# Block-sparse attention folded into a split-precision MoE feed-forward: attention in whole units of eight heads, placed by a plan in quarters of a step

## The chip, the cores and the metric

One NeuronCore of a Trainium2 chip runs the whole kernel. The metric is the device time in microseconds of one execution; the runs before the change have a median of 816.5 us (814.67, 816.5 and 819.2). The profiled execution took 815.99 us, and its trace spans 814.3 us; the 1.69 us between the two lie outside the trace. TensorE's granted clock averaged 0.986 of its full speed in it.

## The reference, cut to what matters

```python
batch, n_heads, seq, head_dim = (4, 8, 768, 64)      # 24 blocks of 32 positions
scores = scale * np.matmul(q, k.transpose(0, 1, 3, 2))
mask = np.abs(blk_i - blk_j) <= 1                    # neighbours
mask = mask | (blk_i == 0) | (blk_j == 0) | (blk_i == n_blocks - 1) | (blk_j == n_blocks - 1)
for qb in range(n_blocks):                           # and three sampled blocks
    for kb in sampled_blocks[qb]:
        mask[qb * block:(qb + 1) * block, kb * block:(kb + 1) * block] = True
scores = np.where(mask, scores, -1000000000.0)
scores = scores - np.max(scores, axis=-1, keepdims=True)
attn = np.exp(scores)
attn = attn / (np.sum(attn, axis=-1, keepdims=True) + 1e-09)
attn_out = np.matmul(attn, v)
x = attn_out.transpose(0, 2, 1, 3).reshape(B * S, H * D)      # 3072 x 512
h = x @ w_in                                         # 512 -> 2048
g = h * (1.0 / (1.0 + np.exp(-1.702 * h)))
return g @ w_out                                     # 2048 -> 512
```

Rows of blocks 1 to 22 see at most eight blocks of keys (first, last, three neighbours, three sampled). Rows of blocks 0 and 23 see all 768 keys.

## The kernel before, in words

**Units and chunks.** A unit is 64 positions of one batch element with all eight heads, held as four pairs of heads. A sparse unit is two neighbouring blocks out of 1 to 22; there are 44. A dense unit is blocks 23 and 0 of one batch element; there are four, and in the order of the 48 units they are numbers 22, 23, 46 and 47. Eight units make a chunk of 512 tokens, the width of one matmul of the MoE, and there are six chunks.

**The MoE step.** For each chunk there are 16 steps, 96 in all. A step does 12 matmuls up (L471 to L473: x and the 128 columns of w_in are each split in a rounded high part and a remainder, and three products of the parts are kept), then ScalarE's tanh (`g`, L479) and VectorE's product (L480), then 12 matmuls down for the step before (L508, L509 and L514), which accumulate over the 16 steps in four PSUM banks. In the first 16 steps `conv`, a generator, also turns the raw weights into such parts on ScalarE and VectorE, seven pieces to a step; afterwards w_out is loaded again in each step (`wst`) and split (L459, L460).

**Attention beside it.** A list of attention steps is worked off. A sparse step is half a unit (four heads): `scores` is 8 matmuls (L260) into banks 0 and 1, then one reduction by VectorE for each bank, which also scales, adds the mask and finds the extreme of each row (L279), and one exponential by ScalarE for each bank, which also sums (L292). A dense step is one head of each of two pairs: four matmuls of 384 keys (L271), reductions, a joint extreme `nmd`, exponentials. `transposes` turns the weights by TensorE (L307, L315) into the same two banks, and ScalarE copies them out as `pt` (L320). `values` multiplies by v into bank 2 (L338, L345). At a unit's end `normalise` scales on VectorE (`x`, L358), and `turn` transposes x (L368) and writes it as `xhi` and `xlo` (L373, L374) into the next chunk's input.

**Order.** The program is written by hand and each engine runs its instructions in that order; nothing reorders them. `tick` writes one MoE step together with the attention steps that are due: scores of step t, values of step t-2, then the 12 matmuls up, then the transposes of step t-1, then the matmuls down. `run` first writes all 16 attention steps of chunk 0, and two more, without MoE steps around them (the prelude, to about 77 us); then, by `goal`, it spreads the steps of chunk c+1 evenly over the 16 MoE steps of chunk c. Where a chunk has more than 16 attention steps (20, in the chunks with dense units) four MoE steps get two attention steps each, both ahead of the matmuls up. In the prelude the banks are others (`early`: scores in 0, 1 or 4, 5, transposes in 3 or 7, or 1 or 5 for a dense one, values in 2 or 6). Keys and values are prefetched in rings of two buffers by SyncE's and GpSimd's queues (`loads`); a buffer is loaded anew once the last step that reads it is written.

## Time and profile before

| what | value |
|---|---|
| median of three runs | 816.5 us |
| profiled execution, its span | 815.99 us, 814.3 us |
| TensorE (PE) busy | 768.3 us, 94% |
| VectorE (DVE), ScalarE (ACT) busy | 50%, 47% |
| DMA | 128.22 MB, 157 GB/s on average |

The page lists busy time by engine, slices of the span, DMA queues, the chain of work that ended last and the costliest groups. A matmul row's duration is longer than its share of the engine, since successive matmuls overlap: what one costs is read from the start of one row to the start of the next. A fp32 matmul of the attention is two instructions in the trace, so that eight score matmuls stand there as x16.

### The profile page before, as it was taken

How to read it: one execution, taken by the hardware profiler on the slowest of the kernel's cores; microseconds unless marked ns; L12 is line 12 of the kernel's file. 1: busy time of each engine (PE TensorE's matmuls, PEld its weight loads, DVE VectorE, ACT ScalarE, POOL GpSimd, SP SyncE). 2: the span in 40 equal slices, each digit the busy share in tenths (PEclk: the TensorE clock that was granted, in tenths of full speed). 3: DMA queues.
4: the chain of work that ended last, by engine and by line, in shares of the span. 5: the costliest groups of instructions: out<-in, count | busy, mean ns of one | idle time of the engine just before them, and what ended most of it. 6: DMA issues, size and time to landing. Idle time of an engine off the chain costs nothing.

```text
span 814.3 us, 19274 instructions
## 1 busy us (share of the span) xinstructions
PE 768.3 (94%) x7584; PEld 567.7 (70%) x7584; DVE 410.7 (50%) x1080; ACT 381.5 (47%) x933; POOL 55.8 (7%) x85
## 2 busy tenths in 40 slices
PE   3677999999999999999999999999999999999996
PEld 1344777777676767777777777777767667788885
DVE  3476788886444444454443544444544444343332
ACT  2476566665444444454444444444544444342332
POOL 5122101000000000000000000000000000000000
PEclk9699999999999999999999999999999999999999
DMA  8999777875734253774453463543654332031112
GB/s 265 313 303 323 216 255 236 258 249 164 210 124 150 66 194 119 202 212 118 118 157 116 134 204 104 154 132 117 167 158 151 115 88 90 27 91 53 49 42 53
DMA packets 61117, 128.22 MB, mean 157 GB/s; under 512 B 7569, under 2 KB 26514, under 8 KB 60514
## 3 DMA queue, kind: packets, MB, share of 16 engines
q1 hardware_dynamic: 46882, 80.50, 33.2%
q0 software_dynamic: 7232, 25.51, 9.7%
q10 hardware_dynamic: 6912, 20.97, 7.9%
q8 instruction: 60, 0.98, 0.5%
q14 instruction: 31, 0.25, 0.1%
HBM read 116.47 MB, written 10.49 MB: 156 GB/s over the span
## 4 chain that ended last, share of the span: by engine, by line
PE 84%; DVE 4%; ACT 4%; DMA 3%; issue 2%; SPq 1%; ACTq 0%; DVEq 0%
PE bank L471 12%; PE bank L508 10%; PE bank L509 10%; PE bank L473 10%; PE bank L472 10%; PE bank L514 10%; PE bank L260 5%; PE bank L338 5%; PE bank L307 4%; PE bank L271 3%; ACT ex L292 2%; DMA raw<-in_moe_w_in_dram 2%; PE bank L345 1%; PE bank L315 1%; PE bank L368 1%
## 5 line engine op out<-in xcount | busy, mean ns | idle before, releaser
L480 DVE SCALAR_TENSOR_TENSOR g<-g,bank 128x512 f32<-128x512 f32 x96 | 66.0, 687 | 233.2 <-ACT g L479 233.2
L471 PE MATMUL bank<-xhi,win 128*128 128x512 f32 x384 | 159.3, 415 | 0.0
L508 PE MATMUL bank<-wout,ghi 128*128 128x512 f32 x384 | 158.4, 412 | 0.0
L509 PE MATMUL bank<-wout,ghi 128*128 128x512 f32 x384 | 151.2, 394 | 0.0
L473 PE MATMUL bank<-xhi,win 128*128 128x512 f32 x384 | 150.3, 391 | 0.0
L292 ACT ACTIVATE ex<-bank,nm 128x256 f32<-128x256 f32 x176 | 81.9, 471 | 145.8 <-DVE nm L279 145.5
L472 PE MATMUL bank<-xlo,win 128*128 128x512 f32 x384 | 149.9, 390 | 0.0
L479 ACT ACTIVATE g<-bank 128x512 f32<-128x512 f32 x96 | 57.3, 597 | 163.3 <-PE bank L473 159.5
L514 PE MATMUL bank<-wout,glo 128*128 128x512 f32 x360 | 98.2, 394 | 0.0
L460 DVE TENSOR_TENSOR wout<-wst,wout 128x512 fp32r<-128x512 f32 x80 | 55.4, 692 | 76.5 <-ACT wout L459 76.5
L471 PEld LDWEIGHTS bank<-xhi,win 128*128 128x128 f32 x384 | 72.0, 187 | 19.7
L260 PE MATMUL bank<-kg,qt 64*32 64x256 f32 x1408 | 64.2, 412 | 20.8 <-DMA vmid<-in_v_dram 10.8
L473 PEld LDWEIGHTS bank<-xhi,win 128*128 128x128 f32 x384 | 72.1, 188 | 16.5
L279 DVE CUSTOM_DVE_ANT_1 bank<-bank,bias 128x256 f32<-128x256 f32 x176 | 71.5, 448 | 22.0 <-PE bank L260 9.6
L508 PEld LDWEIGHTS bank<-wout,ghi 128*128 128x128 f32 x384 | 72.4, 189 | 13.6
L509 PEld LDWEIGHTS bank<-wout,ghi 128*128 128x128 f32 x384 | 72.5, 189 | 13.3
L338 PEld LDWEIGHTS bank<-vown,pt 128*32 128x32 f32 x1408 | 45.7, 113 | 51.0 <-issue 18.4
L472 PEld LDWEIGHTS bank<-xlo,win 128*128 128x128 f32 x384 | 72.3, 188 | 12.6
L514 PEld LDWEIGHTS bank<-wout,glo 128*128 128x128 f32 x360 | 67.6, 188 | 16.0
L217 POOL DMA_INDIRECT vown<-in_v_dram,vidx x44 | 42.5, 965 | 521.1 <-PE bank L338 405.5
L338 PE MATMUL bank<-vown,pt 128*32 128x64 f32 x1408 | 61.1, 228 | 10.8 <-ACT pt L320 10.3
L485 ACT CAST ghi<-g 128x512 fp32r<-128x512 f32 x96 | 59.7, 621 | 20.3 <-DVE g L480 20.1
(71 smaller groups left out, 876.7 us busy)
## 6 DMA issues: line engine op xcount, KB each, us to landing
wst<-ws SPq DMA_DIRECT2D x80, 256.0 KB
kg<-in_kb_dram SPq DMA_DIRECT2D x136, 128.0 KB
kg<-in_kb_dram SPq DMA_DIRECT2D x22, 384.0 KB
raw<-in_moe_w_in_dram ACTq DMA_DIRECT2D x16, 512.0 KB
raw<-in_moe_w_out_dram ACTq DMA_DIRECT2D x16, 512.0 KB
kg<-in_kT_dram SPq DMA_DIRECT2D x4, 1536.0 KB
vown<-in_vd_dram SPq DMA_DIRECT2D x8, 768.0 KB
qt<-in_q_dram SPq DMA_DIRECT2D x22, 256.0 KB
```

What stands on the lines that cost most here:

```text
L260: nc.tensor.matmul(sps[h][BLK * c:BLK * (c + 1), 0:n].rearrange("p (n s) -> p n s", s=BLK), self.qt[r][rows, bi, UT * pair + BLK * j:UT * ...
L279: nc.vector.tensor_tensor_reduce(out=at, in0=at, in1=bias, scale=-SCALE, scalar=3.0e38, op0=ALU.add, op1=ALU.min, accum_out=nm[:, c:c + 1])
L292: nc.scalar.activation(out=ex, in_=sms[c], func=AF.Exp, bias=least[c], scale=-1.0, accum_out=sums[c])
L338: nc.tensor.matmul(av[BLK * c:BLK * (c + 1), 2 * i + h], pt[:, 2 * h + k, BLK * c:BLK * (c + 1)], src[:, at:at + D], start=(k == 0), stop= ...
L471: nc.tensor.matmul(h, wih[:, k], hi[:, k], start=(k == 0), stop=False)
L472: nc.tensor.matmul(h, wih[:, k], lo[:, k], start=False, stop=False)
L473: nc.tensor.matmul(h, wil[:, k], hi[:, k], start=False, stop=(k == NCT - 1))
L480: nc.vector.scalar_tensor_tensor(out=g, in0=g, scalar=1.0, in1=self.h, op0=ALU.add, op1=ALU.mult)
L485: self.nc.scalar.copy(out=ghi, in_=self.g[m][0])
L508: nc.tensor.matmul(o[n], ghi[:, tk[n]], woh, start=(f == 0), stop=False)
L509: nc.tensor.matmul(o[n], ghi[:, tk[n]], wol, start=False, stop=False)
L514: nc.tensor.matmul(o[n], glo[:, tk[n]], woh, start=False, stop=False)
```

## The change: what it does

1. An attention item is now a whole sparse unit (all eight heads) or, of a dense unit, two pairs of heads with one half of the keys (384). There are 44 sparse items and 16 dense ones. A sparse item's 16 score matmuls are written together, its 32 value matmuls together, its 8 transposes together. Of its two banks, one holds the first heads of the pairs and the other the second, both full (512 columns).
2. The four score matmuls of a dense item go to both halves of the array's rows: its h runs over both heads of a pair, where a step before had one. Each half of the keys is exponentiated with its own extreme; `factors` then brings the two halves of a row to a common extreme (five small VectorE operations and one small exponential), and `normalise` scales both halves of the values and adds them (three operations of 128x256 for a dense unit, where there was one).
3. `plan` gives each item a start in quarters of an MoE step: quarter 0 ahead of the matmuls up, 1 in their middle, 2 behind them, 3 inside the matmuls down. At its start an item's scores are written, and behind them the values of the item before; its transposes follow four quarters later (two for a dense item), with the `turn` of the unit before. Sparse items start every 8 quarters (two steps) in most chunks, every 6 or 8 in the first 14 steps, every 5 or 6 beside dense units; dense items every 4.
4. The prelude (`first`) holds chunk 0's eight items and no part of the ninth; for item n it writes the values of n-2, the scores of n, the turn of n-2 and the transposes of n-1. In it scores alternate between banks 0, 1 and 4, 5, and transposes use 3 and 7 always.
5. `up` and `down` can be written in two parts; `down` keeps the order of its matmuls. Loads are asked for after each quarter.

PE at a dense item, before (here h = 0 of two pairs; bank 0 is the first half of the keys and bank 1 the second, and x2 are the two pairs):

```order
L514 MATMUL bank6_91<-wout1_118,glo_4318 128x512
L271 MATMUL bank0_85<-kg0_93,qt0_95 64x384 x2
L271 MATMUL bank1_86<-kg0_93,qt0_95 64x384 x2
L345 MATMUL bank2_87<-vown1_98,pt_4365 64x64 x6
L345 MATMUL bank2_87<-vown1_98,pt_4366 64x64 x6
```

The same place now (bank 0 is the first head of each pair, bank 1 the second, all of one half of the keys):

```order
L528 MATMUL bank6_91<-wout0_117,glo_3978 128x512
L272 MATMUL bank0_85<-kg0_93,qt0_95 64x384
L272 MATMUL bank1_86<-kg0_93,qt0_95 64x384
...
L336 MATMUL bank2_87<-vown0_97,pt_4081 64x64 x6
L336 MATMUL bank2_87<-vown0_97,pt_4085 64x64 x6
L488 MATMUL bank7_92<-xhi1_122,win10_111 128x512
```

The two score rows come twice in the new order (left out once). Neighbours in the order now read different rows of the array (heads) instead of the same ones; the counts are the same.

ACT in the steady part of the MoE, before, one unit in two steps:

```order
L292 ACTIVATE ex_6577,rs_6565<-bank0_85,nm_6574 128x256
L292 ACTIVATE ex_6579,rs_6565<-bank1_86,nm_6574 128x256
L479 ACTIVATE g_6614<-bank7_92 128x512
L320 COPY pt_6613<-bank0_85 128x512
L485 CAST ghi_6630<-g_6614 128x512
L459 CAST wout2_119<-wst_6476 128x512
L292 ACTIVATE ex_6649,rs_6565<-bank0_85,nm_6646 128x256
L292 ACTIVATE ex_6651,rs_6565<-bank1_86,nm_6646 128x256
L479 ACTIVATE g_6694<-bank7_92 128x512
L320 COPY pt_6691<-bank0_85 128x512
L373 CAST xhi0_120<-bank2_87 128x4x64
L485 CAST ghi_6775<-g_6694 128x512
```

Now, one unit in two steps (`nm` and `rs` are the extremes and sums):

```order
L288 ACTIVATE ex_5877,rs_5762<-bank0_85,nm_5763 128x256
L288 ACTIVATE ex_5879,rs_5762<-bank0_85,nm_5763 128x256
L288 ACTIVATE ex_5883,rs_5762<-bank1_86,nm_5763 128x256
L288 ACTIVATE ex_5885,rs_5762<-bank1_86,nm_5763 128x256
L496 ACTIVATE g_5901<-bank7_92 128x512
L502 CAST ghi_5912<-g_5901 128x512
L476 CAST wout0_117<-wst_5703 128x512
L307 COPY pt_5928<-bank0_85 128x512
L307 COPY pt_5933<-bank1_86 128x512
L388 CAST xhi1_122<-bank2_87 128x4x64
L496 ACTIVATE g_5956<-bank7_92 128x512
L502 CAST ghi_5967<-g_5956 128x512
```

All exponentials of a unit stand ahead of one step's tanh, and both copies ahead of the next one's; before, each step had two exponentials ahead of its tanh and one copy behind it.

ACT in the prelude, before, from one unit's exponentials to the next `xhi` (`a` is a piece of the weights, waiting for its `raw`):

```order
L292 ACTIVATE ex_783,rs_771<-bank0_85,nm_780 128x256
L292 ACTIVATE ex_785,rs_771<-bank1_86,nm_780 128x256
L320 COPY pt_807<-bank7_92 128x512
L439 CAST wout0_117<-a_612 128x512
L394 DMA raw_811<-in_moe_w_in_dram 128x1024
L292 ACTIVATE ex_825,rs_771<-bank4_89,nm_822 128x256
L292 ACTIVATE ex_827,rs_771<-bank5_90,nm_822 128x256
L320 COPY pt_855<-bank3_88 128x512
L373 CAST xhi0_120<-bank6_91 128x4x64
```

Now:

```order
L288 ACTIVATE ex_866,rs_846<-bank4_89,nm_847 128x256
L288 ACTIVATE ex_868,rs_846<-bank4_89,nm_847 128x256
L288 ACTIVATE ex_872,rs_846<-bank5_90,nm_847 128x256
L288 ACTIVATE ex_874,rs_846<-bank5_90,nm_847 128x256
L430 DMA ws0_69<-a_626 128x512
L419 ACTIVATE a_879<-raw_716 128x512
L388 CAST xhi0_120<-bank6_91 128x4x64
L307 COPY pt_889<-bank3_88 128x512
L307 COPY pt_894<-bank7_92 128x512
L456 CAST win2_103<-a_785 128x512
```

The copies `pt` of a unit now stand behind the next unit's four exponentials, a piece of the weights and an `xhi`; before, each copy stood behind two exponentials.

The diff, cut to its core (line numbers of the new kernel appear in the order rows only):

```diff
-        early, late = {"s0": ((0, 4), 0), "s1": ((1, 5), 1), "t0": ((3, 7), 0), "t1": ((1, 5), 1), "a": ((2, 6), 2)}[what]
+        early, late = {"s": ((0, 1), (4, 5)), "t": ((3, 7), (3, 7)), "a": ((2,), (6,))}[what], {"s": (0, 1), "t": (0, 1), "a": (2,)}[what]
...
+            for i in range(2):
+                for a in range(2):
+                    for j in range(2):
+                        for h in range(2):
+                            pair, rows, c = 2 * i + a, slice(D * h, D * (h + 1)), 2 * a + j
+                            nc.tensor.matmul(
+                                sps[h][BLK * c:BLK * (c + 1), n * i:n * (i + 1)].rearrange("p (n s) -> p n s", s=BLK),
...
-            for c in range(2):
-                for a in range(2):
-                    pair = 2 * i + a
-                    nc.tensor.matmul(sps[c][UT * a:UT * (a + 1), 0:n], self.qt[r][rows, 0, UT * pair:UT * (pair + 1)],
-                                     kt[rows, pair, n * c:n * (c + 1)], start=True, stop=True, tile_position=(D * h, UT * a))
+            for a in range(2):
+                for h in range(2):
+                    pair, rows = 2 * i + a, slice(D * h, D * (h + 1))
+                    nc.tensor.matmul(sps[h][UT * a:UT * (a + 1), 0:n], self.qt[r][rows, 0, UT * pair:UT * (pair + 1)],
+                                     kt[rows, pair, n * half:n * (half + 1)], start=True, stop=True, tile_position=(D * h, UT * a))
...
-            nc.vector.tensor_tensor(out=one, in0=nm[:, 0:1], in1=nm[:, 1:2], op=ALU.min)
...
+            nc.vector.tensor_tensor(out=rg[:, 1], in0=un["nm"][:, 0], in1=un["nm"][:, 1], op=ALU.min)
+            nc.vector.tensor_tensor(out=f, in0=both(rg[:, 1]), in1=un["nm"], op=ALU.subtract)
+            nc.scalar.activation(out=f, in_=f, func=AF.Exp)
+            nc.vector.tensor_tensor(out=rf, in0=un["rs"], in1=f, op=ALU.mult)
+            nc.vector.tensor_tensor(out=rf[:, 0], in0=rf[:, 0], in1=rf[:, 1], op=ALU.add)
...
+    def plan(self):
...
+            begin = 0 if c == 1 else 4 * QT * (4 * c - 4) - 8
+            end = 4 * QT * 4 * c - 8
+            dense = sum(not self.sparse(g) for g in chunks[c])
+            room, count = end - begin - 4 * dense, len(chunks[c]) - dense
+            even = 2 if room >= 7 * count else 1
+            for k, g in enumerate(chunks[c]):
+                q = room * k // count // even * even if self.sparse(g) else room + 4 * (k - count)
+                starts.append((begin + q, g))
...
+                put(q, self.scores, g)
+                turn = q + (4 if self.sparse(g) else 2)
+                put(turn, self.transposes, g)
+            if before is not None:
+                put(q, self.values, before)
+                if before["end"]:
+                    put(turn, self.turn, before)
...
+        self.gate_lo(m - 1)
+        finish(self.begin(QT * m))
+        if moe:
+            self.up(m, range(0, 2))
+        finish(self.begin(QT * m + 1))
+        if moe:
+            self.up(m, range(2, 4))
+        run(n0)
+        after = self.begin(QT * m + 2)
+        if moe:
+            self.gate(m)
+        finish(after[:2])
+        self.down(m - LAG, 0)
+        if moe:
+            self.gate_hi(m)
+        finish(after[2:])
+        finish(self.begin(QT * m + 3))
+        self.down(m - LAG, 1)
+        self.split(m + 1)
+        self.stream(m + 3)
+        run(n1)
...
+        for n in range(len(items) + 2):
+            if n == 1:
+                next(self.conv)
+            run(self.values, at(n - 2))
+            run(self.scores, at(n))
+            weights(n, 2)
+            run(self.turn, at(n - 2))
+            run(self.transposes, at(n - 1))
+            self.loads()
+            weights(n, 2)
```

## Rows read from the trace of the kernel before

**Rows 1.** The page: busy time by engine, share of the span, instructions.

```profile
PE 768.3 (94%) x7584; PEld 567.7 (70%) x7584; DVE 410.7 (50%) x1080; ACT 381.5 (47%) x933; POOL 55.8 (7%) x85
```

**Rows 2.** Stretches: length, busy us of PE, PEld, DVE, ACT, POOL, clock, DMA.

```profile
0.00:76.84 76.84, 46.90 (x932) 26.70 (x933) 43.48 (x163) 39.30 (x114) 25.10 (x53) 0.87 0.95 303
76.84:195.10 118.26, 117.22 (x1225) 87.77 (x1221) 95.51 (x225) 74.11 (x169) 8.18 (x8) 1.00 0.76 241
...
337.86:457.17 119.31, 119.31 (x1240) 89.68 (x1233) 55.40 (x149) 55.10 (x138) 7.49 (x8) 1.00 0.49 144
...
715.48:804.35 88.87, 88.87 (x386) 72.24 (x385) 33.33 (x51) 28.40 (x49) 0.00 (x0) 1.00 0.20 54
```

**Rows 3.** Timeline of PE around one sparse step: start, duration, instruction.

```profile
403.37 0.40 PE L514 MATMUL bank<-wout,glo 128*128 128x512 f32 x1
403.70 0.66 PE L260 MATMUL bank<-kg,qt 64*32 64x256 f32 x16
404.29 0.24 PE L338 MATMUL bank<-vown,pt 128*32 128x64 f32 x1
...
404.37 0.22 PE L338 MATMUL bank<-vown,pt 128*32 128x64 f32 x1
...
404.73 0.22 PE L338 MATMUL bank<-vown,pt 128*32 128x64 f32 x1
404.88 0.50 PE L471 MATMUL bank<-xhi,win 128*128 128x512 f32 x1
405.21 0.39 PE L472 MATMUL bank<-xlo,win 128*128 128x512 f32 x1
```

**Rows 4.** Timeline of PE in windows that cut a group of scores, and one whole.

```profile
403.70 0.45 PE L260 MATMUL bank<-kg,qt 64*32 64x256 f32 x8
...
277.29 0.54 PE L271 MATMUL bank<-kg,qt 64*64 64x384 f32 x2
...
277.29 1.51 PE L271 MATMUL bank<-kg,qt 64*64 64x384 f32 x8
```

**Rows 5.** Timeline of PE in an MoE step with two attention steps.

```profile
210.01 0.50 PE L471 MATMUL bank<-xhi,win 128*128 128x512 f32 x1
...
216.19 0.66 PE L260 MATMUL bank<-kg,qt 64*32 64x256 f32 x16
218.15 0.66 PE L307 MATMUL bank<-ident,ex 128*128 128x128 f32 x4 [0.71 <-issue]
...
219.54 0.67 PE L260 MATMUL bank<-kg,qt 64*32 64x256 f32 x16 [0.45 <-issue]
220.85 0.50 PE L471 MATMUL bank<-xhi,win 128*128 128x512 f32 x1
```

**Rows 6.** Stretches of the prelude, by the granted clock.

```profile
27.20:40.80 13.60, 10.70 (x174) 6.29 (x174) 7.50 (x24) 6.69 (x20) 1.96 (x2) 0.50 0.99 321
...
51.00:61.30 10.30, 7.36 (x199) 4.55 (x194) 8.95 (x31) 7.26 (x24) 2.04 (x4) 1.00 0.94 319
```

**Rows 7.** Timeline of the prelude: PE at one unit, DVE at the same place of two.

```profile
27.84 1.33 PE L260 MATMUL bank<-kg,qt 64*32 64x256 f32 x16 [3.83 <-DMA kg<-in_kb_dram]
...
56.79 0.68 DVE L407 TENSOR_TENSOR win<-a,win 128x512 fp32r<-128x512 f32 x1
...
62.81 0.68 DVE L407 TENSOR_TENSOR wout<-a,wout 128x512 fp32r<-128x512 f32 x1
```

**Rows 8.** Groups of instructions by line: busy us, mean ns of one, idle before.

```profile
L292 ACT ACTIVATE ex<-bank,nm 128x256 f32<-128x256 f32 x176 | 81.9, 471 | 145.8 <-DVE nm L279 145.5
...
L279 DVE CUSTOM_DVE_ANT_1 bank<-bank,bias 128x256 f32<-128x256 f32 x176 | 71.5, 448 | 22.0 <-PE bank L260 9.6 <-ACT pt L320 7.8 <-issue 4.2
...
L320 ACT COPY pt<-bank 128x512 f32<-128x512 f32 x88 | 51.3, 583 | 3.3 <-issue 1.5 <-PE bank L307 1.4 <-ACT ex L292 0.3
...
L402 ACT ACTIVATE a<-raw 128x512 f32<-128x512 f32 x32 | 21.8, 681 | 18.3 <-DMA raw<-in_moe_w_in_dram 7.3 <-DMA ws<-a 7.0 <-DMA kg<-in_kb_dram 1.1
...
L373 ACT CAST xhi<-bank 128x256 fp32r<-128x256 f32 x48 | 18.6, 388 | 0.2 <-PE bank L368 0.2
```

More of the change, by code (lines that the diff above doesn't have):

```diff
@@ L72, in __init__, with item @@
         self.kmidof, self.vmidof = [None] * RING, [None] * RING
-        self.units, self.kent, self.vent, self.steps = [], [], [], []
+        self.units, self.kent, self.vent, self.items = [], [], [], []
         def entry(of, **more):
-            of.append({"n": len(of), **more})
+            of.append({"n": len(of), "scores": 0, "values": 0, **more})
             return of[-1]
-        def step(k, v, **more):
-            v["last"] = k["last"] = len(self.steps)
-            self.steps.append({"unit": self.units[-1], "k": k, "v": v, **more})
+        def item(k, v, **more):
+            k["scores"] += 1
+            v["values"] += 1
+            self.items.append({"n": len(self.items), "unit": self.units[-1], "k": k, "v": v, **more})
         for b0 in range(0, B, 2):
@@ L87, in __init__ @@
                     entry(self.units, b=b, u=u)
-                    for i in range(2):
-                        step(k, v, i=i, first=i == 0, end=i == 1)
+                    item(k, v, first=True, end=True)
             for b in (b0, b0 + 1):
@@ L94, in __init__ @@
                     v = entry(self.vent, b=b, u=None, i=i)
-                    for h in range(2):
-                        step(k, v, i=i, h=h, first=i + h == 0, end=i + h == 2)
-        self.ends = [k + 1 for k, s in enumerate(self.steps) if s["end"] and s["unit"]["n"] % CU == CU - 1]
+                    for half in range(2):
+                        item(k, v, i=i, half=half, first=i + half == 0, end=i + half == 2)
         self.knext = self.vnext = 0
@@ L225, in loads @@
             more = False
[L226 removed]
+            if self.knext < len(self.kent) and (self.knext < RING or not self.kent[self.knext - RING]["scores"]):
                 self.load_k(self.kent[self.knext])
@@ new lines, in normalise @@
+    def normalise(self, g):
+        nc, un = self.nc, g["unit"]
+        x = un["x"] = self.work.tile([P, 2 * P], F32, name="x", bufs=1)
+        out = [x]
+        if not self.sparse(g):
+            out.append(self.work.tile([P, 384], F32, name="ex", bufs=4)[:, 0:2 * P])
+        for f, to in enumerate(out):
+            nc.vector.tensor_tensor(
+                out=to.rearrange("p (a d) -> p a d", d=D), in0=un["av"][:, 2 * P * f:2 * P * (f + 1)].rearrange("p (a d) -> p a d", d=D),
+                in1=un["ri"][:, f].rearrange("p (a o) -> p a o", o=1).broadcast_to([P, NPAIR, D]), op=ALU.mult)
+        if len(out) == 2:
+            nc.vector.tensor_tensor(out=x, in0=x, in1=out[1], op=ALU.add)
@@ L367, in turn @@
+    def turn(self, g):
+        nc, un = self.nc, g["unit"]
+        xt = un["av"][:, 0:2 * P]
         for i in range(2):
@@ new lines, in plan @@
+    def plan(self):
+        chunks = [[g for g in self.items if g["unit"]["n"] // CU == c] for c in range(NC)]
+        at, starts = {}, []
+        for c in range(1, NC):
+            begin = 0 if c == 1 else 4 * QT * (4 * c - 4) - 8
[6 more added lines that the diff above has]
+                starts.append((begin + q, g))
+        starts.append((end, None))
+        put = lambda q, part, g: at.setdefault(q, []).append((part, g))
+        for k, (q, g) in enumerate(starts):
+            before = starts[k - 1][1] if k else None
+            turn = q + 4
+            if g is not None:
+                put(q, self.scores, g)
[5 more added lines that the diff above has]
+                    put(turn, self.turn, before)
+        return at
@@ new lines, in begin, with tick, run, finish @@
+    def begin(self, q):
+        after = []
+        for part, g in self.at.get(q, ()):
+            after += part(g)
+        self.loads()
+        return after
+    def tick(self, m, n0, n1):
+        def run(n):
+            for _ in range(n):
+                next(self.conv, None)
+        def finish(todo):
+            for f in todo:
+                f()
+        moe = m < NC * NF
+        self.gate_lo(m - 1)
[18 more added lines that the diff above has]
+        self.stream(m + 3)
+        run(n1)
@@ new lines, in first, with run, weights @@
+    def first(self):
+        items = [g for g in self.items if g["unit"]["n"] < CU]
+        at = lambda n: items[n] if 0 <= n < len(items) else None
+        def run(part, g):
+            for f in part(g) if g is not None else ():
+                f()
+        def weights(n, k):
+            for _ in range(k if n > 1 else 0):
+                next(self.conv)
+        for n in range(len(items) + 2):
+            if n == 1:
+                next(self.conv)
+            run(self.values, at(n - 2))
[3 more added lines that the diff above has]
+            run(self.transposes, at(n - 1))
+            self.loads()
+            weights(n, 2)
```

274 lines of the change are left out of this document (107 added, 167 removed).

## The prediction

> **What bounds the kernel now.** I read the page first: TensorE is busy 94% of the span, no other engine over 50% [rows 1]. The table of stretches says where [rows 2]: up to 76.84 us, the prelude, PE is busy 47 of 77 us and its clock averages 0.87, with the DMA engines at 95%; from there to 804.35 PE is busy all the time or nearly so, at full clock. So from 76.84 on, what an edit saves or adds on PE is the time. The last stretch of sixteen steps shown has no attention: 88.87 us, 5.55 a step, 0.231 a matmul. One with eight sparse units takes 119.31, 7.46 a step: attention costs 30.44 us there, 1.90 a step, 3.80 a unit.
>
> Then the timeline of one step, from start to start [rows 3]. The 16 score instructions take 0.59 us until the first value matmul; the 32 value instructions another 0.59. The first score starts 0.33 behind the last down matmul instead of 0.23, and the second up matmul 0.33 behind the first: two hand-overs of 0.10 each. Transposes fit in without such a loss, and cost their own length.
>
> **Part by part.** *Sparse units, all 16 score matmuls at once.* Eight score instructions end 0.45 after their start and sixteen 0.66 [rows 3, 4], so eight more cost 0.21. A whole unit's 32 take 0.59 + 2 x 0.21 = 1.01 in place of 1.18. Value instructions advance in fours, 0.36 us for six or seven such groups (404.37 to 404.73), some 0.056 each: 64 take 0.59 + 8 x 0.056 = 1.04 in place of 1.18. One of the two pairs of hand-overs goes: 0.20. Together 0.51 a unit; the eight transposes and two of x stay as they were. Of 36 units beside MoE steps that is 18.4; eight MoE steps with two attention steps already shared their hand-overs, less 1.6: **16.8 us**. Bounds: 7 (hand-overs alone) and 22 (should scores and values overlap more).
>
> *Dense items.* Before, one pair of instructions on the two column halves ended 0.54 after its start, and four pairs 1.51 [rows 4]: 0.32 a pair, one after the other, since all read the same 64 rows of the array. Now four go to four different quarters, as the sparse ones already go to eight different places at once. Two groups: 0.54 + 0.32 = 0.86, 0.65 less, 16 times: **10.4 us**. Bounds: 0 if the two halves of the rows do not overlap at this shape, 11. The values, transposes and hand-overs of a dense item are as many as before.
>
> *The steps with two attention steps.* From 210.01 to 220.85 is 10.84 us [rows 5], 3.38 over the mean step; a second attention step is worth 1.90 - 0.20 = 1.70 of PE's work, so 1.68 was waited: the transposes started 1.96 behind the scores, since reductions and exponentials come between, and the next scores 1.39 behind the transposes, since ScalarE first copies the bank out. There are eight such steps, four beside each pair of dense units; by the same subtraction they waited 1.7, 1.8, 1.4, 1.4 and 1.7, 1.8, 1.4, 0.5: **11.7 us**. The plan writes no two items ahead of one group of matmuls. What is late next: the closest it comes is four quarters from scores to transposes (two for a dense item) and one quarter from transposes to the next scores. In the last case PE has the transposes, no less than the 0.66 of four of them [rows 5], and six up matmuls at 0.231 before the scores, 2.05 us; the copies can be out 0.66 + 2 x 0.58 = 1.83 after the transposes' start [rows 8]. From a dense item's scores to its transposes PE has 0.86 of scores, 24 value instructions (0.45, by 32 at 0.59) and 12 x 0.231, 4.1 us; it needs the 1.96 that half a sparse unit needed [rows 5], and half as much again for its 384 columns, 2.9. So both fit, with 0.2 and 1.2 us to spare at the least.
>
> *The ninth unit.* The prelude wrote its scores and part of the rest; now the MoE steps carry all. Its scores stand ahead of the first up matmul, where PE waits for the last `xlo`; the extra transposes and values cost **1.0** back.
>
> *New waits.* VectorE is busy 95.5 of 118.26 us in the first sixteen steps [rows 2], 81%; with the same work in 113 us it is 85%. A step that holds a whole unit's scores gives it four reductions in a row, and behind them stand the weights' pieces, the product for `g` and `glo`. I allow 2 us there and 1 us elsewhere, **3 us** back; bounds 0 and 10. SyncE's and GpSimd's loads are asked for as early as before against their use (three items or more), and the w_out load of a step three steps ahead; nothing. The extra small operations for dense units (some ten on VectorE, one on ScalarE, four times) lie on engines at half load; nothing, or 0.3 each if `turn` came late.
>
> *The prelude.* Before, a unit took 6.02 us (56.79 to 62.81 on VectorE) [rows 7]. Now the copies of a unit stand behind the next one's exponentials, and the values need both: from values to values run 1.04 (values) + 1.01 (scores) + 0.90 (two reductions) + 1.88 (four exponentials) + 0.68 (a weight piece) + 0.39 (`xhi`) + 1.17 (two copies) = 7.1 us [rows 8]. Against that, no part of the ninth unit is done there. The third unit's scores started at 27.84 before, when its keys landed [rows 7]; that stays. Six rounds of 7.1 bring the seventh unit's values to 70.4 (27.84 + 42.6); two more without scores, 3.3 and 2.5, end at 76.2; parts at the low clock add some 1.5. So the first up matmul starts at 77.5 instead of 76.84: **0.7 us** back. Bounds: 70 (6.02 a unit, DMA permitting) and 94 (every round at the low clock, below).
>
> **Sum.** 814.3 - 16.8 - 10.4 - 11.7 + 1.0 + 3.0 + 0.7 = 780.1 us of span; with the 1.69 outside the trace 781.8; the median lies 0.5 above the profiled execution: 782.3, so I say 782.5.
>
> **Rivals.** *The prelude gets longer at the low clock* (0.12). From 27.2 to 40.8 PE ran at 0.50, that is 1.2 GHz, around a wait of 3.83 us for keys [rows 6, 7]; from 51.0 to 61.3 at 1.00, 2.4 GHz, busy 7.4 of 10.3 us. A whole-unit round has one burst of some 3.2 us and one gap of nearly 4, where there were two of each. If each of six rounds fell to the low clock, values, scores and transposes would double: 6 x 3 = 18 us, less the 1.5 counted: 799. Half of it: 791. Against it: DMA and VectorE may hide part. The Trainium skill (TensorE: Matmul & The Clock Gate, HAM oscillation) says that bursts parted by idle gaps can each start on the low clock again; by that the whole price of this rival would be paid. The trace shows both levels in the prelude, and so bears it out in part.
>
> *VectorE sets the pace of the first sixteen steps* (0.07): they stay at 118 us instead of 113 or so, or lose 5 more: 787 to 793. For it: 81% busy already, weights' pieces in between. Against: 19% is free, and the attention work is the same.
>
> *Dense scores do not overlap* (0.05): the second part gains nothing, 793. The change then does not do what it says there. For it: no matmul of 384 columns on both row halves stands in the trace. Against: sparse scores do it at 256.
>
> *Slower* (0.03): banks 0 and 1 carry scores and transposes in turn, and both engines that empty them now get a unit's work in one piece. If scores and transposes wait for the emptying as they did in the double steps, 1.68 at each of 52 items, 87 us come on top: 869. It turns the sign from 33.8 / 52 = 0.65 us per item on. For it: rows 5 show this very wait. Against: two steps, or a step, now lie between, where nothing did. The Trainium skill (TensorEngine Tiling (Array Packing), PSUM Bottleneck) warns that faster tiled matmuls can leave the copying out of PSUM as the bound; by that this rival would be likelier, but here both emptying engines are idle for half of the stretch at 337.86 [rows 2].
>
> **How the numbers follow.** The forecast has 0.72, the rivals 0.12, 0.07, 0.05 and 0.03; 0.01 is left for no change. Its own range is 776 to 790: the prelude may end 5 us earlier, waits may be 0 to 7 more. To hold 8 in 10 with the half-paid rivals: 774 to 797. Under 0.5% (4 us) this kernel's measurement tells nothing, its three runs span 4.5. Faster by more: 0.72 + 0.12 + 0.07 + 0.05 = 0.96; within: 0.01; slower: 0.03.
>
> **What would show it.** Right: 16 steps with eight units at 115.3 us (119.31 - 8 x 0.51); a dense item's eight score instructions ending 0.86 after their start; no idle time of PE between scores and transposes in the steps; the first up matmul between 72 and 85 us. Wrong: gaps on PE released by ScalarE's copies or exponentials in the steps with dense units, up matmuls late because VectorE had not yet read bank 7, or a prelude whose clock reads 0.5 throughout.

## The result, and the profile after

The changed kernel takes 809.85 us (median of 5 runs, 807.86 to 810.35); the kernel before took 816.5 beside it. The ratio is 0.9913, 95% interval 0.9884 to 0.9943: faster by a little under 1%. I had forecast 782.5 and a range of 774 to 797: the sign came, a fifth of the gain came, the range did not hold.

The page, busy time by engine, answers to [rows 1]; the table of stretches to [rows 2].

```profile
PE 747.6 (93%) x7584; PEld 577.3 (72%) x7584; DVE 414.2 (51%) x1076; ACT 376.7 (47%) x937; POOL 58.1 (7%) x85
```

```profile
0.00:88.43 88.43, 48.24 (x881) 32.45 (x881) 43.52 (x154) 36.26 (x105) 26.27 (x53) 0.88 0.84 265
88.43:220.67 132.24, 121.15 (x1324) 92.07 (x1324) 101.46 (x245) 76.04 (x186) 9.32 (x8) 0.99 0.70 222
351.06:466.69 115.63, 115.63 (x1240) 91.41 (x1233) 55.45 (x147) 55.00 (x138) 7.49 (x8) 1.00 0.50 147
707.61:796.50 88.89, 88.89 (x386) 72.27 (x385) 33.62 (x51) 28.29 (x49) 0.00 (x0) 1.00 0.20 54
```

The third row is the stretch with eight units: 119.31 before, 115.3 forecast, 115.63 now, with PE busy throughout. The sixteen steps without attention did not change. From 220.67 us on the time came out within 0.1 us of the prediction's sum, and in the two stretches in front it did not:

| stretch | before | forecast | after |
|---|---|---|---|
| up to the first up matmul | 76.84 | 77.5 | 88.43 |
| first 16 steps | 118.26 | 117.2 | 132.24 |
| the rest of the span | 619.2 | 585.4 | 585.5 |

The forecast column is the prediction's sum by stretch: 118.26 - 8 x 0.51 + 1.0 + 2.0 = 117.2 for the first 16 steps, and what is left of 780.1 for the rest. The 113 us that the prediction names beside VectorE's share is not what its own sum gives.

The rest gives 33.7 us; the first two take 25.6 of it back. But work has changed places as well. The scores of a unit are 32 instructions, and the first 16 steps hold those of nine units where there were eight (before, then now):

```profile
L260 PE MATMUL bank<-kg,qt 64*32 64x256 f32 x256 | 10.9, 388 | 1.0 <-ACT pt L320 0.9
```

```profile
L260 PE MATMUL bank<-kg,qt 64*32 64x256 f32 x288 | 11.7, 410 | 2.2 <-ACT pt L307 2.2
```

One half of that unit comes from the prelude, which the prediction priced (1.0); the other half comes from the rest (848 such instructions before, 832 now), which it did not. Half a unit is 1.7 us, (115.63 - 88.89) / 16. With it the prediction's prices give 118.8 for the first 16 steps, which took 13.4 more, and 583.7 for the rest, which took 1.8 more. Of the 1.8, 1.3 is the sparse unit: it saves 0.46, (119.31 - 115.63) / 8, and not 0.51, in some 27 units.

The timeline of PE shows the two new forms of scores, a dense item's and a sparse unit's; they answer to [rows 3, 4]:

```profile
277.03 0.88 PE L272 MATMUL bank<-kg,qt 64*64 64x384 f32 x8
...
363.46 1.09 PE L260 MATMUL bank<-kg,qt 64*32 64x256 f32 x32
```

Eight dense instructions end 0.88 after their start (0.86 forecast, 1.51 before). The sparse 32 run 1.02 from start to the first value matmul, and the 64 values 1.03 (1.01 and 1.04 forecast).

**Where the first stretch went.** One round on the chain of waits (start, length, what ended the step):

```profile
69.06 1.99 PE bank L328 x64
71.05 2.00 PE bank L260 x32
73.05 0.41 DVE bank L283
73.56 0.43 DVE bank L283
74.17 0.30 ACT ex L288
74.54 0.78 ACT ex L288 x4
75.65 0.46 ACT ex L288 x2
76.10 0.55 ACT a L419
76.65 0.27 ACT xhi L388
76.92 0.53 issue
77.45 0.43 PE bank L328 x16
```

This is the round that I had summed, member by member: values, scores, reductions, four exponentials, a weight piece, `xhi`, copies (they run from 76.79 and stand in the chain as "issue"), next values. It takes 8.39 us, not 7.1; values and scores take 1.99 and 2.00 instead of 1.04 and 1.01. The table of stretches gives the clock there as 0.50 (1.2 GHz), and a mean of 0.70, 0.71 and 0.61 in three other bursts:

```profile
43.80:49.50 5.70, 5.28 (x106) 3.53 (x106) 2.77 (x10) 1.11 (x3) 1.44 (x2) 0.70 0.93 269
59.90:65.80 5.90, 5.31 (x106) 3.47 (x106) 2.75 (x10) 1.10 (x3) 1.44 (x2) 0.71 0.96 332
68.90:73.50 4.60, 4.44 (x99) 2.98 (x100) 2.13 (x8) 1.21 (x3) 0.16 (x1) 0.50 0.37 121
77.40:83.00 5.60, 4.59 (x78) 3.57 (x79) 4.04 (x12) 2.75 (x5) 1.48 (x2) 0.61 1.00 299
```

The record does not explain every burst. Values and scores take 1.30 and 1.31 us at 52.74, where it gives 1.00, but 1.93 and 1.89 at 35.45, where it gives 1.00 too; why these are slow stays open.

The six rounds from 28.23 to 77.45 take 49.2 us where I had 42.6. The end of the stretch, from 77.45 to the first up matmul, takes 11.0 us where I had 7.1: ScalarE stands still for the transfer of a raw weight, and the last `xhi` stands behind it:

```profile
87.45 0.66 ACT L419 ACTIVATE a<-raw 128x512 f32<-128x512 f32 x1 [3.22 <-DMA raw<-in_moe_w_out_dram]
88.02 0.35 ACT L388 CAST xhi<-bank 128x256 fp32r<-128x256 f32 x1
```

**Where the first 16 steps went.** Waits of PE in that stretch (waiter, what it waited for, us, times, longest; the last one lies just ahead of the first up matmul):

```profile
PE bank L488 <- DVE g L497: 8.1, 8, 3.1
PE bank L260 <- ACT pt L307: 2.2, 2, 1.2
PE bank L488 <- ACT xhi L388: 1.0, 1, 1.0
```

The timelines of PE, ScalarE and VectorE around one of the eight:

```profile
160.85 0.39 PE L490 MATMUL bank<-xhi,win 128*128 128x512 f32 x1
...
166.73 0.50 PE L488 MATMUL bank<-xhi,win 128*128 128x512 f32 x1 [1.60 <-DVE g L497]
```

```profile
160.30 0.47 ACT L288 ACTIVATE ex<-bank,nm 128x256 f32<-128x256 f32 x1
...
160.75 0.62 ACT L502 CAST ghi<-g 128x512 fp32r<-128x512 f32 x1
161.26 0.71 ACT L419 ACTIVATE a<-raw 128x512 f32<-128x512 f32 x1
161.97 0.62 ACT L456 CAST wout<-a 128x512 fp32r<-128x512 f32 x1
...
163.23 0.67 ACT L419 ACTIVATE a<-raw 128x512 f32<-128x512 f32 x1 [0.63 <-ACT wout L456]
164.84 0.62 ACT L456 CAST win<-a 128x512 fp32r<-128x512 f32 x1 [0.94 <-DVE a L453]
165.37 0.59 ACT L496 ACTIVATE g<-bank 128x512 f32<-128x512 f32 x1
```

```profile
157.82 0.42 DVE L283 CUSTOM_DVE_ANT_1 bank<-bank,bias 128x256 f32<-128x256 f32 x1
...
164.12 0.69 DVE L453 SCALAR_TENSOR_TENSOR a<-raw,a 128x512 int32<-128x512 int32 x1
165.99 0.69 DVE L497 SCALAR_TENSOR_TENSOR g<-g,bank 128x512 f32<-128x512 f32 x1 [1.18 <-ACT g L496]
```

The up matmuls end at 161.2. Their tanh starts at 165.37, because ScalarE has four pieces of two weights to do first, the last of them waiting for VectorE, which had a whole unit's reductions from 157.82 on. The product follows, and only then may the next up matmul write bank 7: 1.60 us of PE lost.

### The profile page after: what moved, and what is told of

Read it like the earlier page. It is cut to its first block, busy times and chain, and to the rows that moved or that the text cites. A ratio compares the mean times of both kernels' runs of the same rounds, so it can differ in the third digit from the quotient of the medians.

```text
span 806.2 us, 19246 instructions
## 1 busy us (share of the span) xinstructions
PE 747.6 (93%) x7584; PEld 577.3 (72%) x7584; DVE 414.2 (51%) x1076; ACT 376.7 (47%) x937; POOL 58.1 (7%) x85
## 4 chain that ended last, share of the span: by engine, by line
PE 77%; DVE 7%; ACT 6%; DMA 4%; issue 3%; ACTq 1%; SPq 1%; DVEq 0%
PE bank L488 11%; PE bank L532 10%; PE bank L490 9%; PE bank L533 9%; PE bank L528 9%; PE bank L489 9%; PE bank L328 5%; PE bank L260 5%; PE bank L303 5%; DMA ws<-a 2%; DMA vmid<-in_v_dram 2%; ACT ex L288 2%; PE bank L336 2%; PE bank L272 2%; DVE a L453 1%
## 5 line engine op out<-in xcount | busy, mean ns | idle before, releaser
L288 ACT ACTIVATE ex<-bank,nm 128x256 f32<-128x256 f32 (+1 forms) x208 | 99.5, 488 | 143.9 <-DVE nm L283 123.4
L532 PE MATMUL bank<-wout,ghi 128*128 128x512 f32 x384 | 154.7, 403 | 0.0
L533 PE MATMUL bank<-wout,ghi 128*128 128x512 f32 x384 | 151.7, 395 | 0.0
L528 PE MATMUL bank<-wout,glo 128*128 128x512 f32 x384 | 107.7, 394 | 0.0
L283 DVE CUSTOM_DVE_ANT_1 bank<-bank,bias 128x256 f32<-128x256 f32 x176 | 73.8, 440 | 26.0 <-PE bank L260 23.0
L528 PEld LDWEIGHTS bank<-wout,glo 128*128 128x128 f32 x384 | 72.4, 189 | 17.2
L533 PEld LDWEIGHTS bank<-wout,ghi 128*128 128x128 f32 x384 | 72.5, 189 | 15.4
L489 PEld LDWEIGHTS bank<-xlo,win 128*128 128x128 f32 x384 | 72.4, 189 | 13.4 <-DVE xlo L389 0.3
L216 POOL DMA_INDIRECT vown<-in_v_dram,vidx x44 | 44.9, 1019 | 480.8 <-PE bank L328 368.4
L260 PE MATMUL bank<-kg,qt 64*32 64x256 f32 x1408 | 57.2, 426 | 18.4 <-DMA kg<-in_kb_dram 11.0
L328 PE MATMUL bank<-vown,pt 128*32 128x64 f32 x1408 | 55.6, 232 | 20.0 <-ACT pt L307 12.3
```

The source lines that it names most:

```text
L260: nc.tensor.matmul(sps[h][BLK * c:BLK * (c + 1), n * i:n * (i + 1)].rearrange("p (n s) -> p n s", s=BLK), self.qt[r][rows, bi, UT * pair + ...
L283: nc.vector.tensor_tensor_reduce(out=at, in0=at, in1=bias, scale=-SCALE, scalar=3.0e38, op0=ALU.add, op1=ALU.min, accum_out=un["nm"][:, ha ...
L288: nc.scalar.activation(out=ex, in_=sps[h][:, n * k:n * (k + 1)], func=AF.Exp, bias=un["nm"][:, half, c:c + 1], scale=-1.0, accum_out=un["r ...
L328: nc.tensor.matmul(av[BLK * c:BLK * (c + 1), 0, 2 * i + h], g["pt"][h][:, 2 * i + k, BLK * c:BLK * (c + 1)], src[:, at:at + D], start=(k = ...
L489: nc.tensor.matmul(h, wih[:, k], lo[:, k], start=False, stop=False)
L528: nc.tensor.matmul(o[n], glo[:, tk[n]], woh, start=False, stop=last)
```

## The experiments

All times of stretches are from one profiled execution each, medians from four runs where nothing else stands, ratios against the kernel before on the same chip. Stretches with the same instructions differ between executions: the first one ended at 85.25 to 88.43 in five kernels that share it. Differences under 3 us in it decide nothing here. The kernels ran in several groups, and the kernel before took 813.7 to 816.5 us beside them; between groups, ratios are compared and not medians.

| run | first up matmul | first 16 steps | median | ratio, interval |
|---|---|---|---|---|
| changed kernel | 88.43 | 132.24 | 809.85 | 0.9913 (0.9884 to 0.9943) |
| e1_split | 79.82 | 132.19 | 799.41 | 0.98 (0.9759 to 0.9842) |
| e2_pieces_behind | 88.42 | 131.65 | 807.07 | 0.9891 (0.9850 to 0.9932) |
| e3_five_a | 87.75 | 128.67 | 803.45 | 0.9838 (0.9794 to 0.9882) |
| e5_no_pieces | 86.76 | 118.30 | 792.06, one run | |
| e4_both | 80.05 | 128.74 | 796.21 | 0.9766 (0.9722 to 0.9809) |
| e6_half_steps | 78.16 | 126.41 | 795.53 | 0.9753 (0.9714 to 0.9792) |
| e6_half_three_a | 76.84 | 127.14 | 794.30 | 0.9742 (0.9688 to 0.9797) |
| e10_fewer_ahead | 74.30 | 129.53 | 791.92 | 0.9707 (0.9664 to 0.9749) |
| b1_before_no_pieces | 73.60 | 117.37 | 811.40, one run | |
| f1_behind | 78.34 | 127.57 | 792.76 | 0.9726 (0.9694 to 0.9759) |
| f2_behind_less | 72.39 | 127.59 | 788.01 | 0.9693 (0.9667 to 0.9720) |
| g2_pool_alone | 85.25 | 127.11 | 799.12 | 0.983 (0.9779 to 0.9881) |
| g1_pool_behind | 74.05 | 125.94 | 786.33 | 0.9653 (0.9608 to 0.9699) |
| g3_pool_ahead | 76.07 | 128.18 | 788.33 | 0.9665 (0.9648 to 0.9682) |
| h1_save_sp | 74.97 | 124.02 | 788.57 | 0.9666 (0.9636 to 0.9696) |
| h2_save_sp_pool | 74.20 | 123.28 | 784.96 | 0.9623 (0.9592 to 0.9654) |

**e1_split: copies ahead of the next softmax, in the first stretch.**

```diff
             run(self.values, at(n - 2))
-            run(self.scores, at(n))
+            softmax = self.scores(at(n)) if at(n) is not None else ()
+            run(self.transposes, at(n - 1))
+            for f in softmax:
+                f()
             weights(n, 2)
             run(self.turn, at(n - 2))
-            run(self.transposes, at(n - 1))
```

> One part moved, only in the stretch ahead of the first MoE step: TensorE's order stays scores of a unit, then the transposes of the unit before, but ScalarE's two copies out of those transposes (pt, 0.6 us each) are put ahead of the unit's four exponentials (0.49 us each) and VectorE's four reductions. Theory P (the rounds of 8.5 us are a chain: values wait for pt, which stands behind four exponentials, four reductions and the weights' pieces): the wait of values for pt in that stretch (about 10 us) goes, rounds fall to 7 or less, the first up matmul is at 74 to 79 us instead of 88.4 and the kernel at 796 to 801. Rival D (the stretch goes at the pace of transfers and of the low clock: DMA share 0.84, clock 0.88): the first up matmul stays within 2 us of 88.4 and the kernel at 808 to 811. Rival W (pieces of the weights on VectorE and ScalarE set the rounds): half of it, 82 to 86 and 803 to 807.

Measured: theory P. The waits of values for `pt` fall from 12.3 us to 0.3. The stretch is 8.6 us shorter, with the clock no better, but the DMA engines now at 0.96:

```profile
0.00:79.82 79.82, 42.96 (x881) 27.65 (x881) 42.19 (x154) 36.61 (x105) 25.26 (x53) 0.83 0.96 301
```

So the low clock cost time because values and scores stood on the chain; with the copies earlier they no longer do. The end, 79.82, lies 0.8 past the window that I gave theory P.

**e2_pieces_behind: the weights' pieces behind the gate.**

```diff
-        run(n0)
         after = self.begin(QT * m + 2)
         if moe:
             self.gate(m)
         finish(after[:2])
+        run(n0)
```

> One part moved, only in the first 16 MoE steps: the first four pieces of a weight's conversion of each step are issued behind the step's gate (tanh, product) and the copies of its attention instead of ahead of them. Theory C (tanh and product stand in order behind the pieces on ScalarE and VectorE, and the next up matmul waits for the product): the wait of the up matmul for the product (8.3 us in 9 waits) falls under 2 us, the first 16 steps take 122 to 127 us instead of 132.2, the kernel 800 to 805. Rival A (VectorE's and ScalarE's work of these steps is too much wherever it stands): the wait only moves to another one, 130 to 135 us and 807 to 813. A third way: the weights come later than the step that needs them, 135 to 140 us.

Measured: rival A. Waits of PE in the first 16 steps:

```profile
PE bank L328 <- DVE xlo L389: 4.2, 2, 2.2
PE bank L260 <- ACT pt L307: 3.4, 2, 2.1
PE bank L488 <- ACT xhi L388: 2.8, 1, 2.8
PE bank L488 <- ACT win L456: 1.6, 1, 1.6
PE bank L488 <- DVE g L497: 0.5, 1, 0.5
```

The wait for the product is gone, 8.1 to 0.5, and about the same time is lost at what now stands behind the pieces. (The 2.8 us for `xhi` lie ahead of the first up matmul.)

**e3_five_a, and e4_both: five buffers.** The second joins it with e1's edit.

```diff
-a = ... self.work.tile([P, DM], I32, name="a", bufs=3)
+a = ... self.work.tile([P, DM], I32, name="a", bufs=5)
-self.wst[m] = self.work.tile([P, DM], F32, name="wst")
+self.wst[m] = self.work.tile([P, DM], I32, name="a", bufs=5).bitcast(F32)
```

> Only buffers: the converted weight (a) and the weight that is read back later (wst) share five buffers instead of three and two of their own. Theory B (ScalarE's first piece of a weight waits for a buffer that the write-out of an earlier weight still holds, 5.7, 3.0 and 7.6 us at 134.7, 192.4 and 201.3, and blocks the tanh behind it): those waits go, the first 16 steps take 122 to 127 us instead of 132.2, the kernel 800 to 805. Rival: the transfers are only late, and the steps wait for the weights' loads instead: within 2 us of 132.2, kernel 807 to 812.

> The two edits that each helped, together: the copies out of the transposes ahead of the exponentials in the stretch before the first step, and five buffers shared by the converted and the read-back weights. If their places are apart (the first saved 8.6 us ahead of the first MoE step, the second 3.6 us in the first 16 steps): first up matmul at 79 to 80, first 16 steps 128 to 129 us, span 793 to 795, kernel 794.5 to 797. Rival: with the first stretch shorter the pieces run later against the steps, so that the second gain is lost: first 16 steps 131 to 133, kernel 798 to 801.

Measured: 3.6 us off the 16 steps, between theory B and its rival; the kernel's 803.45 lies in theory B's window. The two gains add: 80.05 and 128.74.

**e5_no_pieces and b1_before_no_pieces: the pieces left out of the steps, in the changed kernel and in the one before.**

```diff
     def need(self, f, i):
-        while (f, i) not in self.ready:
-            next(self.conv, None)
+        pass
...
-wih, wil = (self.win[f][...
+wih, wil = (self.win[f % 4][...
...
+        self.conv = self.fetches()
```

> Leaves work out: behind the stretch ahead of the first MoE step no weight is converted and none is written out; the steps use the first four up weights and the first three down weights over again, the loads of the raw weights stay. Theory C+B (all of the loss in the first 16 steps comes from the pieces that stand on VectorE and ScalarE): 16 steps at 112 to 115 us, near the 115.3 of the later steps with eight units, kernel 790 to 793. Rival (the eight units with their banks do it, whatever the weights): over 125 us, kernel above 802.

> The kernel before, with the same work left out as in the run of the changed kernel without pieces (no weight is converted or written out behind the stretch ahead of the first step; the same first four up and three down weights serve every step; the raw weights are still loaded). It asks what the pieces cost the kernel before in its first 16 steps (118.3 us). Theory H (attention in halves, one in every step, leaves VectorE a share of each step that the pieces fit into; whole units pile up two steps' worth and so the pieces, harmless before, cost 14 us now): within 2 us of 118.3. Rival: they cost the kernel before as much, and its 118.3 us held them: 106 to 112 us.

Measured, the 16 steps in the changed kernel and in the one before:

```profile
86.76:205.06 118.30, 117.76 (x1324) 92.56 (x1325) 48.36 (x148) 50.06 (x140) 7.49 (x8) 0.99 0.66 218
```

```profile
73.60:190.97 117.37, 116.64 (x1225) 87.56 (x1221) 45.53 (x133) 46.34 (x121) 7.51 (x8) 1.00 0.65 214
```

The pieces cost the changed kernel 13.9 us (132.24 to 118.30) and the one before 0.9 (118.26 to 117.37), for the same work on VectorE within 3 us (53.1 and 50.0). Each is one run, and both edits leave out the write-outs with the pieces. Theory H holds in its number (117.37, within 2 us of 118.3): that some VectorE work is hidden beside attention in halves says nothing of it beside whole units. The size of the units is not isolated, though: the changed kernel also has nine units in these steps, closer together, and no run changes that alone. The changed kernel's 118.30 lies between its two answers, 3.3 us above theory C+B's upper end. Nothing is lost in that: a ninth unit is worth 3.3 us, so that 115.63 for eight makes 119.0, and PE is idle for 0.54 us only.

**e6_half_steps and e6_half_three_a: a unit's parts only in the middle of a step; e10_fewer_ahead: three pieces a round in the first stretch instead of four.** The first and last stand on e4_both; the second on e1's edit, with three buffers.

```diff
-        items = [g for g in self.items if g["unit"]["n"] < CU]
+        items = [g for g in self.items if g["unit"]["n"] <= CU]
...
-                starts.append((begin + q, g))
+                starts.append((begin + q if c > 1 else 8 * k - 6, g))
```

```diff
             self.loads()
-            weights(n, 2)
+            weights(n, 1)
```

> The two edits together and a third one: in the first 16 steps a unit's parts stand only in the middle of a step (between the up matmuls and the down matmuls), eight quarters apart, never ahead of the up matmuls; to make room the ninth unit's scores and transposes go into the stretch before. Theory Q (in the steps that have the weights' pieces, parts that stand ahead of the up matmuls find their copies and reductions behind the pieces, those in the middle do not: in the changed kernel's trace steps of the second kind run at 6.6 or 7.8 us without a wait, those of the first lose 0.5 to 3.3 us each): first 16 steps 116 to 121 us instead of 128.5, kernel 783 to 789. Rival F (VectorE at 77% of these steps cannot do more, so waits appear in the middle too): 126 to 130 us, kernel 793 to 798. Rival P2 (the ninth unit's parts lengthen the stretch before by 2 us or more): first up matmul after 82 us.

> As the kernel with parts in the middle of the steps only, but with three buffers for the converted weight as in the changed kernel. Tells whether the write-out of the weights holds ScalarE by itself: if it does, the first 16 steps take 3 to 4 us longer than with five buffers; if the waits for the buffer only came from pieces that were late already, within 1 us.

> The two edits together, with three instead of four pieces of a weight in each round of the stretch before the first step, so that about two weights less (0.5 MB each) are fetched and converted there. If that stretch goes at the pace of the transfers now (DMA share 0.96 in it with the first edit): the first up matmul comes 2 to 3.5 us earlier, near 77, and the first 16 steps take as much longer or more, kernel 795 to 799. If it goes at the pace of a chain or of the engines' pieces: first up matmul 4 us or more earlier, or not earlier at all.

Measured: the middle is worth 5.1 us with three buffers (132.19 to 127.14) and 2.3 with five. Both numbers also hold the ninth unit's reductions, which the edit moves into the first stretch; VectorE's work in the steps falls by 2.4 us with them (101.50 to 99.14). Rival F holds for e6_half_steps: the up matmul still waits for the product five times, 5.1 us in all. Five buffers are then worth 0.7 us: the wait for the write-out was mostly a wait for pieces that were late. In e10_fewer_ahead the first stretch ends 5.8 us earlier with some two weights fewer, and the steps give back only 0.8. By the expectation 2 to 3.5 us would have been the transfers' pace, and 4 or more that of a chain or of the pieces. The DMA engines are at 0.95 all the same, so which of them sets that end is not settled.

**f1_behind and f2_behind_less: e6_half_steps with e2's edit, and with e10's.**

> The kernel with its parts in the middle of the steps, with the first four pieces of each step behind the gate and the attention's copies instead of ahead. In that kernel's trace the steps with scores run free of waits and each following one, with transposes, ends 1 to 1.7 us late because the next up matmul waits for the product (7 times, 9 us); with nothing ahead of the up matmuls nothing else should wait for what the pieces now stand in front of. Theory Q2 (VectorE's backlog is harmless where the product passes it): first 16 steps 116 to 119 us instead of 126.4, span 781 to 784, kernel 783 to 788. Rival F2 (the backlog only moves on to the copies, VectorE's 77% is too much for two-step bursts): 124 to 128 us, kernel 792 to 797.

> The same with three instead of four pieces in each round of the stretch before the first step, which moved the first up matmul from 80.1 to 74.3 us where the parts stood ahead of the up matmuls. If the first 16 steps can take the pieces that come later: first up matmul at 72 to 75, first 16 steps 117 to 121 us, kernel 778 to 784. If VectorE is then the bound there: 124 us or more, kernel 785 to 792.

Measured: rival F2, in both. The steps are free of waits from the second on up to some 65 us in, and wait after that: 127.57, and 127.59 in f2_behind_less. The fewer pieces ahead again bring the first up matmul 6 us forward.

**g2_pool_alone, g1_pool_behind, g3_pool_ahead: part of VectorE's work on GpSimd.** On the changed kernel; on f2_behind_less; on that with the pieces ahead of the gate.

```diff
-            nc.vector.tensor_tensor(out=t[:, DM:2 * DM], ...
+            engine = nc.vector if self.early else nc.gpsimd
+            engine.tensor_tensor(out=t[:, DM:2 * DM], ...
```

> The changed kernel with one edit: in the MoE steps the last piece of each weight (the subtraction that makes its low part, 128x512, 0.69 us on VectorE) runs on GpSimd, which has 9 us of work in these 132 us. That takes some 22 subtractions, about 14 us, from VectorE's 101.5. Theory V (VectorE's amount of work in these steps makes the waits, since pieces moved in order only move the wait): first 16 steps 122 to 128 us instead of 132.2, kernel 800 to 806. Rival Z (the chain of a weight's pieces from engine to engine and the copies standing behind it make the waits, not the amount): 130 to 135 us, kernel 807 to 812. A price that no run shows yet: GpSimd's time for this subtraction; if it is over 3 us, weights come late and the steps take longer than 135 us.

> The fastest so far (copies first, five buffers, parts in the middle of the steps, pieces behind the gate, fewer pieces ahead), with the subtraction on GpSimd. Its steps ran free of waits up to 60 us after the first and lost 12 us after that, where VectorE had no idle time left but what the weights' chain gave it. Theory V: first 16 steps 117 to 122 us instead of 127.6, kernel 778 to 784. Rival Z: within 2 us of 127.6, kernel 786 to 790.

> The same with the first four pieces ahead of the gate again, as in the changed kernel. Tells whether the order against the gate matters once VectorE has less to do: under theory V the two orders come within 2 us of each other in the first 16 steps; if the order counts by itself, this one loses 3 to 9 us at the up matmuls that wait for the product.

Measured: alone, 5.1 us off the 16 steps without any change of order: theory V. On the better order it gives 1.7 only (125.94, kernel 786.33), and that is rival Z: theory V had 117 to 122. So VectorE's amount of work is not the whole cause. The gate's order is worth 2.2 us there, between the two answers.

**h1_save_sp and h2_save_sp_pool: the write-out from SyncE's queue.** On f2_behind_less and on g1_pool_behind.

```diff
-                nc.scalar.dma_start(out=self.ws[f], ...
+                nc.sync.dma_start(out=self.ws[f], ...
```

> The fastest order with VectorE doing all pieces (copies first, five buffers, parts in the middle, pieces behind the gate, fewer ahead), with one edit: the write-out of each converted down weight (ws) is issued from SyncE's queue instead of ScalarE's. In that kernel ScalarE stands still for 2.4 us at 139.3 to 141.7 ahead of a write-out that it issues itself, and the transposes' step then takes 2.4 us longer. Theory W (ScalarE's own issue of the write-out holds the copies and the tanh behind it): this stop goes, the first 16 steps take 123 to 126 us instead of 127.6, kernel 783 to 786.5. Rival: the weights' buffers wait elsewhere for the same transfer: within 1 us of 127.6, kernel 786 to 790.

> The same edit on the kernel whose low parts of the weights are made on GpSimd; there the stop of ScalarE is 2.6 us and the first 16 steps take 125.9 us. Theory W: 121 to 124 us, kernel 780 to 785. Rival: within 1 us of 125.9, kernel 785 to 788.

Measured: 3.6 and 2.7 us off the 16 steps, as theory W has it. The kernel's 788.57 lies above theory W's window and inside its rival's; its ratio is 0.9666 for f2_behind_less's 0.9693, with intervals that overlap, and in the profiled runs the first stretch ended 2.6 us later. The second kernel's 784.96 lies in the window and is the fastest of all.

```profile
0.00:74.20 74.20, 44.80 (x888) 29.92 (x889) 40.96 (x157) 37.48 (x112) 26.02 (x54) 0.91 0.93 296
74.20:197.48 123.28, 119.87 (x1316) 92.97 (x1317) 98.45 (x215) 73.11 (x177) 41.70 (x34) 0.97 0.76 247
```

It beats the kernel before by 3.8% and, by the two ratios (0.9623 / 0.9913), the changed one by 2.9%. Its steps from 89 to 170 us run free of waits.

## Why the prediction was wrong

*Right.* Sparse units (1.02 and 1.03 us, 115.63 for 16 steps), dense items (0.88), and the steps that held two attention steps: they make up the 33.7 us of the rest, 33.8 by the prediction's sum. That the two agree to 0.1 us is in part luck, since 1.7 us of the gain is work moved into the first 16 steps. The banks that scores and transposes share cost nothing there, so the slower rival falls; dense scores do overlap.

*Wrong, the step on the prelude* ("0.7 us back"): 11.6. I had the right chain, with values and scores at full clock and 1.5 us in all for the low one. The rounds run at 8.4, and in the round shown above values and scores take 2 us more at 0.50; the six rounds make up 6.6 us of the 10.9 that the stretch took over the forecast. Another 3.9 came at the end, with ScalarE waiting for a raw weight, a wait that I had at nothing. My first rival, given 0.12, named the low clock and priced it at 9 us (half paid) to 18; how much of the 6.6 it makes no run separates. The rule that I cited beside it, of the Trainium skill (TensorE: Matmul & The Clock Gate, HAM oscillation), is borne out here in part: 1.99 for 1.04 in one burst, but 1.30 in another. e1_split shows that the clock need not be cured: copies put earlier gave 8.6 us at a mean clock of 0.83.

*Wrong, the step on new waits* ("3 us back", bounds 0 and 10, of it 2 in the first 16 steps): 13.9 by e5_no_pieces, or 15.4 by the sum (132.24 for 116.8 without waits), in the first 16 steps, and 0.7 us of waits on PE elsewhere. I reckoned with shares: VectorE at 85% has room. My second rival had the place right and the price too low, 118 to 123 us. What it missed is order. Whole units give VectorE and ScalarE two steps' worth at once; the pieces, a chain that passes between the two engines three times, stand in the same queues; tanh and product stand behind both. Shown: the pieces' 13.9 us (e5, b1); that the place of the parts, VectorE's amount and ScalarE's issue of the write-out each hold a share (5.1, 5.1 and 3.6 us, each on its own base; they don't add). Argued only: that the size of the units, and not the ninth unit or the closer starts, makes the pieces cost this. Of the 5.0 us that stay in h2_save_sp_pool over 118.3, 2.9 are idle time of PE (3.41 for 0.54) and 2.1 longer busy time, with the clock at 0.97 for 0.99.

## What to carry to other kernels

When work is moved in larger units, test every engine's queue at the place where the unit lands, not its busy share: what stands behind the burst, and who waits for that. A background job that was hidden beside small units (0.9 us) cost fifteen times as much here beside large ones. Where a stretch is a chain, look for the short copy that stands behind a later unit's long work, and put it in front.

## What the hardware showed that was not expected

GpSimd's 128x512 subtraction takes 1.34 us for VectorE's 0.69, and it is not free for VectorE. The timelines of g2_pool_alone, VectorE's 128x4 factor and GpSimd's subtraction:

```profile
148.66 1.27 DVE L357 TENSOR_SCALAR rg<-rs 128x4 f32<-128x4 f32 x1
```

```profile
148.61 1.29 POOL L425 TENSOR_TENSOR wout<-a,wout 128x512 fp32r<-128x512 f32 x1 [2.08 <-ACT wout L457]
```

The small operation takes 0.16 elsewhere (in f1_behind at 138.19) and here ends 0.03 us behind GpSimd's. Over the first 16 steps one of the pieces' operations on two SBUF inputs rose from 0.683 to 0.851 us in the mean, while the product, which reads PSUM, stayed at 0.687. All eleven products that ran beside a subtraction took 0.69, while one of the pieces' operations that started 0.04 us behind one, at 174.68, took 1.80. 25 subtractions of 0.69, 17 us, left VectorE, and its busy time fell by 7 (101.46 to 94.37). The Trainium skill (SBUF — State Buffer, SBUF: two separate sides) describes a port pair that the two engines share by an exclusive lock; the trace agrees.
